# Eight PSUM tiles of one bank behind the attention, and in the attention part a re-planned order and another narrowing of the weights

## The chip, the cores and the metric

One core of one Trainium2 chip runs the whole program in one launch. The metric is the device time of that launch in microseconds (us); a version's time is the median of several runs. The engines are TensorE (PE, with PEld its weight load), VectorE (DVE), ScalarE (ACT), GpSimd (POOL) and SyncE (SP), which only issues DMAs here. They run side by side and wait for each other by semaphores.

## The reference, cut to what matters

The inputs come as float64; the kernel computes in fp32 and in products of two rounded halves.

```python
# q, k, v: (4, 12, 448, 64);  d_model 768;  conv kernel 5;  feed-forward width 3072
def reference(q, k, v, w_val, conv_w, w_out, g_ln, w_ch1, w_ch2):
    x = causal_softmax(q @ k.T / 8) @ v                 # -> (4, 448, 768)
    gate = sigmoid(sum(conv_w[i] * shift(x, 4 - i) for i in range(5)))
    x = (gate * (x @ w_val)) @ w_out
    xn = (x - mean(x)) / sqrt(var(x) + 1e-6) * g_ln
    return x + relu(xn @ w_ch1) @ w_ch2                 # float32
```

## The kernel before

**Four stages follow each other, and each keeps TensorE as full as it can.** The attention stage takes 24 pairs of heads (4 batches of 6). For a pair PE computes the scores (L372, with the last 64 rows in L341 or L347), DVE adds the mask and finds the row maximum (L394), ACT takes exp and the row sum (L400), DVE turns the sums into reciprocals (L403, L404), POOL scales the rows (L408), PE transposes (L443), ACT copies out of PSUM (L446) and PE multiplies with v (L467, L472). The result of a pair goes three ways: ACT copies it to SBUF (L475), POOL splits it into a high and a low half (L238, L479), and DVE runs the convolution over it out of PSUM (L485). When a batch is complete, 36 groups of three products with w_val follow (L599) and DVE multiplies with the gate (L609). These products are laid between the pairs of the next batch; those of the last batch stand alone at the end.

**w_val and w_out are narrowed in this stage.** They arrive as float64, one block of 128 x 768 at a time, 12 blocks in all (`narrow_steps`). The exponent is moved by integer operations on the two 32-bit words: three passes on DVE (L243, L245, L247), an absolute value on ACT (L256), a fourth pass on DVE that zeroes what is too small (L259), then a cast to the high half on ACT (L236) and the low half by a subtraction on POOL (L525).

**The second stage** (`tile_steps`) multiplies 14 tiles of 128 rows with w_out (L812), takes mean and variance on DVE (L827, L835, L836), the inverse root on POOL (L839), keeps the unnormalised row for the residual (ACT L830), normalises (ACT L842), transposes on PE (L848), scales with g_ln on DVE (L851) and forms seven left or right operands of a Strassen-like scheme (L866, L867, sums in L712). **The third stage** multiplies these with w_ch1 (L1038), which is narrowed beside it with a scaled-magnitude variant: ACT L283 takes the absolute value scaled by 2^-112, which is already the shifted exponent, and three DVE passes follow (L264, L266, L268) and no fourth. PSUM sums are copied or added out of PSUM (ACT L1050, DVE L1053), go through a relu on ACT (L1009) and are stored to DRAM by DMAs that ACT issues (L1014). **The fourth stage** multiplies with w_ch2 (L1154); DVE splits its wide weight blocks (L1099) and adds each product to the accumulator (L1165).

**PSUM** has eight banks. Behind the attention they are held as four tiles `Z` of two banks each; the tile's first half and second half are the rings A, B, C of the later stages, and a whole tile is the output `o` of a second-stage tile or its transposed rows `x`.

**The order of the work is written out by a planner.** `Plan.arrange` plays the program through with a cost for each task and engine and picks, at each step, the ready task with the earliest due time. The kernel is then emitted in that order, and every engine and DMA queue works its list in order. The later stages give `lock=True` and a table `TUNE` of shifts to due times, one per kind of task: the planner then also keeps apart tasks marked `hog` on DVE and POOL, and takes pipelining and shorter semaphore hops into account. The attention stage is planned without that, with one due time for each kind of task (`DUE`). `HOME` says for the small sums (L712) whether DVE or POOL takes them.

Of the kernel before, what the change touches and what calls it, by code (L numbers as in the profile page):

```python
# [8 lines left out]
F32 = mybir.dt.float32  # L9
# [17 lines left out]
TUNE = {'eld': -26.4, 'ea': -8.5, 'eb0': 2.2, 'eb1': -4.7, 'es3': -0.8, 'eh0': -6.9, 'eo0': -12.4, 'eh1': 1.6, 'eo1': 22.2, 'es2': -6.7, 'eh2': -9.3, 'eo2': 3.2, 'eh3': -7.7, 'eo3': 10.0, 'eh4': -1.3, 'eo4': 9.9, 'es4': -9.5, 'eh5': -2.9, 'eo5': 22.5, 'eh6': -24.6, 'eo6': 11.2, 'est': 17.6, 'yld': -33.4, 'ylo': 17.2, 'ka': -21.4, 'xst': -15.6, 'km': -1.5, 'kr': 52.9, 'kn': -10.5, 'kt': 0.0, 'fx': 19.4, 'Xh0': 7.8, 'Xl0': 8.6, 'Xh5': -21.6, 'Xl5': 23.0, 'Xt1': -7.7, 'Xh6': 31.9, 'Xl6': 3.3, 'Xh1': 6.1, 'Xl1': 22.0, 'Xt2': -10.7, 'Xh2': -8.2, 'Xl2': 0.0, 'Xt3': -19.7, 'Xt4': -16.1, 'Xh3': -12.7, 'Xl3': 16.1, 'Xh4': -1.1, 'Xl4': 7.2, 'Zh0': 5.7, 'Zl0': -11.5, 'Zh5': -28.2, 'Zl5': -10.8, 'Zh6': 10.5, 'Zl6': -13.0, 'Zh1': 35.6, 'Zl1': -37.2, 'Zt2': 5.3, 'Zh2': -3.9, 'Zt3': -7.3, 'Zt4': -28.4, 'Zh3': 21.6, 'Zl3': -16.3, 'Zh4': 1.4, 'Zl4': -37.8, 'w1ld': -5.7, 'r1': 30.1, 'w0a': 17.9, 'w0b0': -12.7, 'w0b2': -3.0, 'w1a': -3.7, 'w1b0': -22.5, 'w1b1': 48.5, 'w1b2': -4.9, 'ws1': -19.1, 'ws3': -8.1, 'wh0': 3.7, 'wo0': 14.6, 'wh1': 19.8, 'wo1': -10.9, 'ws2': 11.2, 'wo2': 15.3, 'wh3': -5.4, 'wh4': 3.6, 'wo4': -15.0, 'ws4': -19.0, 'wh5': 15.6, 'wh6': -22.4, 'wo6': 16.8, 'r2': 18.1, 'u1a': -5.4, 'u1l': 4.4, 'u1b1': 0.1, 'u0l': 31.4, 'u0b1': -5.2, 'wd5': -4.2, 'wd6': 22.3, 'wd0': -2.9, 'T3': -8.3, 'T1': -19.9, 'T4': 18.6, 'wd3': -28.8, 'wd1': -14.4, 'wd2': -1.6, 'wd4': -4.3, 'cp00': -5.9, 'cp10': 11.5, 'cp20': 14.2, 'ad30': 57.6, 're30': 11.0, 'cp01': -17.8, 'cp21': -28.8, 'ad31': -25.7, 're31': 7.4, 'st31': 5.6, 'ad40': -31.7, 're40': -4.3, 'st40': -15.7, 'ad41': 21.4, 're41': -10.0, 'st41': 0.9, 'ad50': -21.4, 're50': 21.1, 'st50': -15.0, 'ad51': 9.9, 're51': 1.9, 'st51': -2.8, 're60': -3.5, 'st60': 3.9, 're61': 0.1, 'st61': 18.1, 'accld': 29.3, 'sgld': -7.3, 'whi0': -8.5, 'whi1': 16.9, 'wlo1': 14.6, 'whi2': 12.7, 'wlo2': -15.7, 'whi3': -34.1, 'wlo4': -9.1, 'whi5': -6.2, 'wlo5': -5.3, 'whi6': -9.0, 'wlo6': 24.9, 'rld': -18.1, 'sm0': 12.5, 'sm2': 59.3, 'sm3': -4.0, 'clo0': -1.0, 'clo1': 0.3, 'clo2': -7.3, 'clo3': 19.2, 'chi4': 2.8, 'clo4': -42.7, 'chi5': -5.8, 'clo5': -14.6, 'chi6': 8.6, 'clo6': -8.8, 'ac0': 0.4, 'ac1': -15.8, 'ac2': -1.0, 'ac4': -13.6, 'ac5': 43.0, 'ac6': -25.5, 'eb2': 16.3, 'es1': 31.4, 'yhi': -17.3, 'ks': 7.2, 'nm': -7.6, 'Zt1': -3.1, 'Zl2': -14.1, 'w0b1': -1.2, 'wh2': 3.5, 'wo3': 15.4, 'wo5': -5.9, 'u1b0': -21.8, 'u0a': -28.2, 'u0b0': -15.0, 'st30': 15.9, 'cp11': -1.2, 'wlo3': 3.4, 'whi4': -1.3, 'sm1': 0.6, 'chi0': -0.9, 'chi1': 0.2, 'chi2': 30.1, 'chi3': 18.9, 'ac3': 22.8, 'T2': 4.4, 'wlo0': -14.2}  # L27

HOME = {'es1': 'DVE', 'es3': 'POOL', 'es2': 'POOL', 'es4': 'DVE', 'Xt1': 'DVE', 'Xt2': 'DVE', 'Xt3': 'POOL', 'Xt4': 'POOL', 'Zt1': 'POOL', 'Zt2': 'POOL', 'Zt3': 'POOL', 'Zt4': 'DVE', 'ws1': 'POOL', 'ws3': 'DVE', 'ws2': 'POOL', 'ws4': 'POOL', 'T3': 'DVE', 'T1': 'DVE', 'T2': 'DVE', 'T4': 'POOL', 'sm0': 'DVE', 'sm1': 'POOL', 'sm2': 'DVE', 'sm3': 'DVE'}
# [23 lines left out]
class Plan:  # L53
# [6 lines left out]
    SWITCH = 95  # L60
# [21 lines left out]
    def task(self, cost, fn, due, after=(), new=(), uses=(), lag=0, mode=None, hog=False, behind=None, key=None):  # L82
        due += self.tune.get(key, 0)
        if key in self.home:
            cost = {self.home[key]: {'POOL': 1040, 'DVE': 554}[self.home[key]]}

        def run():
            for b in new:
                b.tile = self.place(b)
            fn(k.engine)  # L90

        k = Task(cost, run, due, after, new, uses, lag, mode, hog, behind)
        self.tasks.append(k)
        return k
# [86 lines left out]
def f32(ap):  # L181
    return ap.bitcast(F32)
# [3 lines left out]
def attention_gate_ffn(  # L186
# [98 lines left out]
    with ExitStack() as ph1:  # L285
# [41 lines left out]
        plan = Plan(pools, DUE["same"])  # L327
# [7 lines left out]
        def shared(n, raws, need):  # L335
# [15 lines left out]
            if len(raws) == 1:  # L351
                t = task({"PE": 720}, whole, n + DUE["sc"], need, banks, raws, mode="full")
            else:
                t = task({"PE": 800}, sides, n + DUE["sc"], need, banks, raws, mode="quad")
# [3 lines left out]
        def pair(n):  # L358
# [3 lines left out]
            lq = task({"SP": 900}, dma(lambda: raw.tile, qk[b, c]), n + DUE["lq"], new=[raw], lag=2500)  # L362
            lv = task({"SP": 500}, dma(lambda: v_t.tile, v[b, 2 * c:2 * c + 2].rearrange("h p c d -> p h c d")),
                      n + DUE["lv"], new=[v_t], lag=2500)
# [9 lines left out]
            t01 = task({"PE": 760}, lambda e: scores(e, (0, 1), s01), n + DUE["s01"], [lq, chain["s"]], s01, [raw], mode="row")  # L374
            t2 = task({"PE": 640}, lambda e: scores(e, (2,), s2), n + DUE["s2"], [t01], s2, [raw], mode="row")
# [3 lines left out]
        def weights(n, first, last):  # L379
# [58 lines left out]
            for i, (blocks, need, dst, at) in enumerate(banks):  # L438
# [9 lines left out]
                tt = task({"PE": 440}, turn, n + DUE["turn"] + 0.05 * i, need, [bank], list({b for b, _ in blocks}), mode="full")  # L448
                (tc_ if at is None else te).append(task(
                    {"ACT": 480}, evac, n + DUE["evac"] + 0.05 * i, [tt], [dst] if not at else [], [bank, dst] if at else [bank]))  # L450
            return pt, te, [cpt for _, cpt in ends], tc_

        def rest_of_pair(n, first, own, ends):
# [7 lines left out]
            def attend(e):  # L461
# [6 lines left out]
                for kc in range(NQ + 1):  # L468
                    for h in range(2):
# [4 lines left out]
            ta = task({"PE": 1815}, attend, n + DUE["attend"], [lv, *te, *tc_], [pv], [v_t, pt, *cpts], mode="col")  # L474
            cx = task({"ACT": 430}, lambda e: nc.scalar.copy(x.tile, pv.tile[:, :S]), n + DUE["x"], [ta], [x], [pv])  # L475
            tg = task({"POOL": 610}, lambda e: nc.gpsimd.tensor_scalar(g.tile, x.tile, cw[:, c, KT - 1:KT], 1.0, ALU.mult, ALU.mult),  # L476
                      n + DUE["g"], [cx, tcw], [g], [x])
            th = task({"POOL": 645}, lambda e: cast_hi(xh.tile, x.tile, nc.gpsimd), n + DUE["xh"], [cx], [xh], [x])
            tl = task({"POOL": 1115}, lambda e: nc.gpsimd.tensor_tensor(xl.tile, x.tile, f32(xh.tile), ALU.subtract),  # L479
                      n + DUE["xl"], [th], [xl], [x, xh])  # L480
            last = tg
            for t in range(KT - 1):
# [6 lines left out]
                last = task({"DVE": 715}, conv, n + DUE["conv"] + 0.01 * t, [last], [], [pv, g])  # L489
            return xh, xl, g, tl, last  # L490

        def narrow_steps(c):
# [7 lines left out]
            ld = task({"SP": 3800}, load, due - 0.7, new=[raw], lag=2500)  # L500
# [9 lines left out]
            ops = narrow_ops  # L510

            def bits(i):
                def fn(e):
                    if i == 0:
                        dst["ops"] = ops(raw.tile, w.tile)
# [723 lines left out]
```

## Time and profile before

| what | value |
|---|---|
| median of 3 runs | 1007.7 us (1007.18 to 1008.37) |
| the profiled execution's own time | 1007.35 us |
| its span from first to last instruction | 1005.6 us |
| PE busy, x instructions | 963.7 us (96%), 5731 |
| PEld busy | 857.0 us (85%) |
| DVE busy | 765.0 us (76%), 1549 |
| ACT busy | 561.6 us (56%), 1153 |
| POOL busy | 294.5 us (29%), 367 |

Busy means that an instruction of the engine was under way. A matmul overlaps the one behind it and its end is modelled, so PE busy is no measure of PE at its peak; time in which PE is not busy is a stall for certain. The chain of work that ended last lies on PE for 72% of the span and on DVE for 14%. The granted clock of TensorE was 0.998 of full speed over the span.

### The profile page before, as it was taken

The numbers are of one execution on the slowest core, as the hardware profiler recorded it, in microseconds if no ns is written. First come the engines' busy times: TensorE is split into PE (matmuls) and PEld (weight loads), VectorE is DVE, ScalarE is ACT, GpSimd is POOL, SyncE is SP. The second block draws the span as 40 slices with busy tenths as digits, with TensorE's granted clock in tenths as the row PEclk, the third lists the DMA queues.
The fourth block names the chain that finished last, engine by engine and source line by source line (L and its number), as shares of the span: only waits on it lengthen the run. The fifth ranks groups of instructions, "written<-read, shape, count | busy, mean of one in ns | idle before, by whom it ended". The sixth has DMA issues, their size and how long they took to land.

```text
span 1005.6 us, 16427 instructions
## 1 busy us (share of the span) xinstructions
PE 963.7 (96%) x5731; PEld 857.0 (85%) x5731; DVE 765.0 (76%) x1549; ACT 561.6 (56%) x1153; POOL 294.5 (29%) x367
## 2 busy tenths in 40 slices
PE   9989999999999989999979999999999999999998
PEld 5657777788999978888868878888999999999998
DVE  6899989864488876666667776667999888979873
ACT  7988878862365556666555556564445335334330
POOL 5888877671032231111111121110110000100100
PEclk9999999999999999999999999999999999999999
DMA  6344445322554467878787877689725424424322
GB/s 199 118 158 146 153 154 164 113 83 87 160 173 143 141 225 249 254 222 264 244 251 250 271 223 237 207 265 321 272 84 179 145 63 157 134 82 147 126 95 95
DMA packets 115474, 177.26 MB, mean 176 GB/s; under 512 B 10432, under 2 KB 87744, under 8 KB 115392
## 3 DMA queue, kind: packets, MB, share of 16 engines
q1 hardware_dynamic: 70704, 154.19, 46.3%
q10 hardware_dynamic: 44688, 22.03, 7.5%
q8 instruction: 45, 0.74, 0.3%
q14 instruction: 37, 0.30, 0.1%
HBM read 118.39 MB, written 57.80 MB: 175 GB/s over the span
## 4 chain that ended last, share of the span: by engine, by line
PE 72%; DVE 14%; POOL 4%; DMA 3%; ACT 3%; issue 3%; SPq 0%; ACTq 0%; DVEq 0%; POOLq 0%
PE z L1154 28%; PE z L1038 24%; PE val L599 5%; PE z L812 5%; PE t L443 2%; PE pv L467 2%; PE s L599 2%; DVE g L485 2%; PE s L372 2%; POOL p L408 2%; DVE p L394 1%; DVE x L867 1%; DVE lf L1053 1%; DMA lf<-in_w_ch 1%; DMA hd<-lf 1%
## 5 line engine op out<-in xcount | busy, mean ns | idle before, releaser
L1038 PE MATMUL z<-x,ar 128*128 128x512 f32 (+1 forms) x1224 | 256.5, 368 | 15.4 <-DVE lf L1053 6.3
L1038 PEld LDWEIGHTS z<-x,ar 128*128 128x128 f32 x1224 | 222.9, 189 | 46.5 <-ACT lf L1050 7.9
L712 POOL TENSOR_TENSOR lf<-lf 128x384 f32<-128x384 f32 x52 | 59.4, 1142 | 332.7 <-DVE lf L712 162.3
L1154 PE MATMUL z<-x,x 128*128 128x384 f32 x684 | 125.4, 335 | 1.8 <-DVE lf L1165 0.8
L1165 DVE TENSOR_TENSOR acc<-z,acc 128x384 f32<-128x384 f32 x168 | 91.6, 552 | 46.6 <-PE z L1154 45.4
L1154 PEld LDWEIGHTS z<-x,x 128*128 128x128 f32 x684 | 118.8, 188 | 3.5 <-issue 1.8
L1136 ACT CAST x<-lf 128x384 fp32r<-128x384 f32 x102 | 51.3, 513 | 87.3 <-PE z L1154 67.2
L812 PE MATMUL z<-wo,ar 128*128 128x384 f32 x504 | 91.2, 337 | 0.4 <-DVE ar L801 0.4
L812 PEld LDWEIGHTS z<-wo,ar 128*128 128x128 f32 x504 | 87.0, 188 | 1.1 <-DVE ar L801 0.9
L1154 PE MATMUL z<-x,ar 128*128 128x384 f32 x468 | 85.4, 334 | 0.4 <-ACT ar L1136 0.4
L408 POOL TENSOR_SCALAR p<-p,r 128x128 f32<-128x128 f32 (+1 forms) x144 | 78.4, 567 | 22.4 <-DVE r L404 21.4
L1154 PEld LDWEIGHTS z<-x,ar 128*128 128x128 f32 x468 | 81.4, 188 | 0.7 <-issue 0.7
L400 ACT ACTIVATE p<-p,negm 128x128 f32<-128x128 f32 (+1 forms) x144 | 71.9, 504 | 12.5 <-DVE negm L394 11.7
L485 DVE SCALAR_TENSOR_TENSOR g<-pv,cw,g 128x444 f32<-128x444 f32 (+1 forms) x96 | 64.7, 674 | 11.0 <-POOL g L476 9.0
L1050 ACT COPY lf<-z 128x512 f32<-128x512 f32 (+1 forms) x72 | 37.6, 535 | 52.7 <-PE z L1038 52.0
L1038 PE MATMUL z<-x,w 128*128 128x512 f32 (+1 forms) x288 | 61.8, 366 | 1.4 <-DVE lf L1053 1.4
L1137 DVE TENSOR_TENSOR x<-lf,x 128x384 fp32r<-128x384 f32 x102 | 59.6, 594 | 3.2 <-DMA af<-wd 1.6
L1009 ACT ACTIVATE lf<-lf 128x512 f32<-128x512 f32 (+1 forms) x72 | 41.6, 577 | 36.4 <-DVE lf L1053 32.8
L1038 PEld LDWEIGHTS z<-x,w 128*128 128x128 f32 x288 | 52.4, 188 | 8.6 <-ACT lf L1009 1.8
L1136 ACT CAST ar<-lf 128x384 fp32r<-128x384 f32 x57 | 28.7, 513 | 52.9 <-PE z L1154 43.6
L1053 DVE TENSOR_TENSOR lf<-z,lf 128x512 f32<-128x512 f32 (+1 forms) x72 | 43.5, 618 | 16.5 <-PE z L1038 15.7
L753 DVE TENSOR_TENSOR ar<-lf,ar 128x384 fp32r<-128x384 f32 x62 | 38.1, 619 | 22.8 <-ACT ar L751 22.2
(152 smaller groups left out, 1855.3 us busy)
## 6 DMA issues: line engine op xcount, KB each, us to landing
lf<-in_w_ch SPq DMA_DIRECT2D x31, 768.0 KB, 5.7
af<-wd SPq DMA_DIRECT2D x28, 576.0 KB, 4.9
lf<-hd SPq DMA_DIRECT2D x19, 768.0 KB, 4.4
raw<-in_qk SPq DMA_DIRECT2D x24, 512.0 KB, 4.6
hd<-lf ACTq DMA_DIRECT2D x48, 256.0 KB, 4.1
af<-in_w_ch SPq DMA_DIRECT2D x15, 768.0 KB, 5.2
wd<-af SPq DMA_DIRECT2D x60, 192.0 KB, 3.2
hd<-lf ACTq DMA_DIRECT2D x48, 192.0 KB, 4.5
```

The lines of the kernel that those rows point to most:

```text
L400: nc.scalar.activation(reg, reg, AF.Exp, bias=negm.tile[:, i:i + 1], scale=-1.0, accum_out=ssum.tile[:, i:i + 1])
L408: nc.gpsimd.tensor_scalar(reg, reg, r.tile[:, i:i + 1], 1.0, ALU.mult, ALU.mult)
L485: nc.vector.scalar_tensor_tensor(g.tile[:, d:], pv.tile[:, :S - d], cw[:, c, t:t + 1], g.tile[:, d:], ALU.mult, ALU.add)
L599: nc.tensor.matmul(ps.tile[:, :S], w[:, do, kc * P:(kc + 1) * P], x.tile, start=(kc == 0 and i == 0), stop=(kc == KC - 1 and i == 2),)
L712: ENG[eng].tensor_tensor(o, a, b, op)
L812: nc.tensor.matmul(o.tile[:, nh, :HALF], y.tile[:, kc], wo_t[kc][:, a, nh * HALF:(nh + 1) * HALF], start=(count[nh] == 0), stop=(count[nh] ...
L1038: nc.tensor.matmul(b.tile[:, :width], w.tile[:, a, kc], X[g][p][:, c, kc], start=(m == 0 and fresh), stop=(m == 3 * JJ - 1), skip_group_ch ...
L1053: ka = task({"DVE": 154 + int(1.04 * width)}, lambda e: nc.vector.tensor_tensor(q.tile, b.tile[:, :width], q.tile, ALU.add), t1, [k], [], ...
L1136: k_hi = task({"ACT": 514}, lambda e, src=src, h=h: nc.scalar.copy(h.tile[:, 0], src()), due, [need, k_hi], [h], [buf], key=f"chi{i}")
L1137: k = task({"DVE": 554}, lambda e, src=src, h=h: nc.vector.tensor_tensor(h.tile[:, 1], src(), f32(h.tile[:, 0]), ALU.subtract), due + 1, [ ...
L1154: nc.tensor.matmul(b.tile[:, :HALF], h.tile[:, a, jj], w.tile[:, c, jj], start=(n == 0 and fresh), stop=(n == 3 * JJ - 1), skip_group_chec ...
L1165: k = task({"DVE": 554}, lambda e: nc.vector.tensor_tensor(acc(), b.tile[:, :HALF], acc(), ALU.add), t0 + UNIT + 0.2, [k, acc_ld[u]], [], ...
```

## The change

Five things are changed.

1. In the attention stage the planner is called with `lock=True` and a table `TUNE1` of 267 shifts, one for each kind of task in each batch. The costs of the attention's tasks are other numbers (the row maximum 150 + 1.05 w ns in place of 78 + 1.042 w, exp 385 + 0.81 w in place of 284 + 0.83 w, the reciprocals 390 in place of 310, an evacuation 586 in place of 480, and so on), and the tasks on POOL, the reciprocals and the narrowing are marked `hog`. The order in which the engines get their instructions is thereby another one.
2. `narrow_steps` uses the scaled-magnitude variant of the third stage: one ACT pass (L283's form) and three DVE passes. The ACT absolute value in place and the fourth DVE pass (L256, L259) go.
3. `Z` becomes four pairs of tiles of one bank each. What read or wrote both halves in one instruction is split in two: the copy for the residual (L830), the normalisation (L842) and the scaling with g_ln (L851). The statistics and the transposes address the two tiles.
4. In the planner the small sums cost 1095 ns on POOL in place of 1040, the wide split of L1099 costs 1350 in place of 1260, and a change of PE mode 85 in place of 95.
5. `TUNE` and `HOME` of the later stages are other tables: 164 of 190 shifts differ, and 10 of 24 small sums change engine.

```diff
-    SWITCH = 95
+    SWITCH = 85
...
-            cost = {self.home[key]: {'POOL': 1040, 'DVE': 554}[self.home[key]]}
+            cost = {self.home[key]: {'POOL': 1095, 'DVE': 554}[self.home[key]]}
...
-        plan = Plan(pools, DUE["same"])
+        plan = Plan(pools, DUE["same"], lock=True, tune=TUNE1)
...
-            tr = task({"DVE": 310}, inverse, n + DUE["inv"], tx, [r], [ssum])
+            tr = task({"DVE": 390}, inverse, n + DUE["inv"], tx, [r], [ssum], hog=True, key=f"inv{b}")
...
-                tn.append(task({"POOL": 240 + int(0.83 * w)}, lambda e, a=(i, buf, o, w): norm(e, *a),
-                               n + DUE["norm"] + 0.02 * i, [tr], [], [buf, r]))
+                tn.append(task({"POOL": 230 + int(0.86 * w)}, lambda e, a=(i, buf, o, w): norm(e, *a),
+                               n + DUE["norm"] + 0.02 * i, [tr], [], [buf, r], hog=True, key=f"nrm{b}_{i}"))
...
-            k = ld
-            for i, ns in enumerate((590, 990, 875)):
-                k = task({"DVE": ns}, bits(i), due + 0.01 * i, [k], [w] if i == 0 else [], [raw] if i == 0 else [raw, w], hog=True)
-            ab = task({"ACT": 815}, lambda e: narrow_abs(raw.tile), due + 0.04, [k], [], [raw])
-            k = task({"DVE": 870}, lambda e: narrow_2(raw.tile, w.tile), due + 0.05, [ab], [], [raw, w], hog=True)
-            hi = task({"ACT": 738}, lambda e: cast_hi(parts()[0], w.tile, ENG[e]), due + 0.06, [k], [], [w])
-            lo = task({"POOL": 1800}, lambda e: ENG[e].tensor_tensor(parts()[1], w.tile, f32(parts()[0]), ALU.subtract),
-                      due + 0.07, [hi], [], [w])
+            k = task({"ACT": 915}, lambda e: scaled(raw.tile, w.tile), due - 0.01, [ld], [w], [raw], key=f"na{c // 3}")
+            for i, ns in enumerate((558, 957, 957)):
+                k = task({"DVE": ns}, bits(i), due + 0.01 * i, [k], [], [raw, w], hog=True, key=f"nb{i}_{c // 3}")
+            hi = task({"ACT": 837}, lambda e: cast_hi(parts()[0], w.tile, ENG[e]), due + 0.06, [k], [], [w], key=f"nh{c // 3}")
+            lo = task({"POOL": 1820}, lambda e: ENG[e].tensor_tensor(parts()[1], w.tile, f32(parts()[0]), ALU.subtract),
+                      due + 0.07, [hi], [], [w], hog=True, key=f"no{c // 3}")
...
-        Z = [ps.tile([P, 2, 512], F32, name=f"z{i}") for i in range(4)]
+        Z = [[ps.tile([P, 512], F32, name=f"z{i}_{h}") for h in range(2)] for i in range(4)]
...
-            ka = task({"ACT": 800}, lambda e: nc.scalar.copy(stage.tile.rearrange("p (a f) -> p a f", a=2), o.tile[:, :, :HALF]),
+            def kept(e):
+                for nh in range(2):
+                    nc.scalar.copy(stage.tile[:, nh * HALF:(nh + 1) * HALF], o.tile[nh][:, :HALF])
+
+            ka = task({"ACT": 870}, kept,
...
+            def normed(e):
+                for nh in range(2):
+                    nc.scalar.activation(xn.tile[:, nh * HALF:(nh + 1) * HALF], o.tile[nh][:, :HALF], AF.Identity, bias=nm.tile, scale=rs.tile)
+
+            kn = task({"ACT": 1080}, normed, D(n - 2), [km], [xn], [nm, rs, o], key="kn")
...
+            def scale(e):
+                for q in range(2):
+                    nc.vector.tensor_tensor(fx.tile[:, q], x.tile[q][:, :QU].rearrange("p (c f) -> p c f", f=P),
+                                            g_t[:, q * JJ:(q + 1) * JJ, None].to_broadcast([P, JJ, P]), ALU.mult)
+
+            return task({"DVE": 1024}, scale, D(n - 1), [kt_], [fx], [x], key="fx")
...
-                w_made[kk, i] = task({"DVE": 1260}, lambda e, sg=sg, b=b: nc.vector.tensor_tensor(
+                w_made[kk, i] = task({"DVE": 1350}, lambda e, sg=sg, b=b: nc.vector.tensor_tensor(
```

## Rows read from the trace of the kernel before

**Rows 1.** Busy us (instructions) by stretch: PE, PEld, DVE, ACT, POOL; clock, DMA share, GB/s.

```profile
0.00:20.00 20.00, 17.98 (x81) 10.22 (x83) 14.46 (x68) 14.77 (x50) 10.11 (x25) 1.00 0.67 225
20.00:130.00 110.00, 100.53 (x861) 71.66 (x858) 98.15 (x271) 96.15 (x260) 95.97 (x134) 1.00 0.41 138
130.00:256.00 126.00, 125.28 (x934) 99.62 (x933) 88.28 (x226) 80.98 (x208) 75.76 (x106) 1.00 0.35 119
256.00:357.00 101.00, 96.35 (x580) 94.75 (x578) 80.56 (x164) 56.48 (x92) 25.77 (x28) 1.00 0.50 159
357.00:685.00 328.00, 314.04 (x1520) 275.94 (x1521) 217.57 (x329) 190.52 (x329) 58.11 (x49) 0.99 0.78 245
685.00:1006.00 321.00, 309.54 (x1764) 304.82 (x1762) 266.01 (x494) 122.71 (x219) 28.76 (x27) 1.00 0.42 143
```

**Rows 2.** Chain that ended last, in order of time (start us, us, what): attention's last products.

```profile
233.40 21.91 PE s L599 x108
```

**Rows 3.** Waits of PEld from 20 to 130 us: us in total, times, longest us.

```profile
PEld pv L467 <- DVE g L485: 6.5, 7, 1.5
```

**Rows 4.** Groups of DVE from 20 to 130 us: count, busy us, mean ns, idle before.

```profile
L259 DVE SCALAR_TENSOR_TENSOR wt<-wraw,wt 128x768 f32<-128x768 f32 x7 | 8.0, 1149 | 0.0
...
L245 DVE SCALAR_TENSOR_TENSOR wt<-wraw,wt 128x768 uint32<-128x768 uint32 x6 | 7.2, 1193 | 0.1
...
L403 DVE TENSOR_TENSOR r<-ssum,tiny 128x6 f32<-128x6 f32 (+2 forms) x13 | 5.2, 397 | 0.0
...
L243 DVE TENSOR_SCALAR wt<-wraw 128x768 uint32<-128x768 uint32 x6 | 4.9, 815 | 0.5 <-POOL wvl L525 0.5
```

**Rows 5.** Timeline from 55 to 69 us: start us, us, instruction, idle before and its releaser.

```profile
57.22 1.82 POOL L525 TENSOR_TENSOR wvl<-wt,wvh 128x768 fp32r<-128x768 f32 x1
...
57.75 1.31 DVE L403 TENSOR_TENSOR r<-ssum,tiny 128x8 f32<-128x8 f32 x1
...
59.90 1.51 PE L467 MATMUL pv<-pt,v 128*64 128x384 f32 x12 [1.30 <-DVE g L485]
```

**Rows 6.** The line of the reciprocals over the whole span: ns shortest/median/longest.

```profile
L403 DVE TENSOR_TENSOR r<-ssum,tiny x24: 151/163/1306, 11.2 to 214.0; 128x6 f32<-128x6 f32 x9, 128x8 f32<-128x8 f32 x9, 128x7 f32<-128x7 f32 x6
```

**Rows 7.** Groups by form over the whole span: narrowing passes of either variant.

```profile
L256 ACT ACTIVATE wraw<-wraw 128x768 f32<-128x768 f32 x12 | 11.2, 935 | 0.0
...
L266 DVE SCALAR_TENSOR_TENSOR lf<-lf 128x768 uint32<-128x768 uint32 x15 | 14.3, 956 | 0.3
```

**Rows 8.** Groups by form: the second stage's whole-tile operations and a 384-wide evacuation.

```profile
L1050 ACT COPY lf<-z 128x384 f32<-128x384 f32 x36 | 17.4, 482 | 28.7 <-PE z L1038 28.5
...
L842 ACT ACTIVATE af<-z,nm,rs 128x768 f32<-128x768 f32 x14 | 13.9, 992 | 9.3 <-DVE nm L840 9.3
...
L851 DVE TENSOR_TENSOR af<-z,g_t 128x768 f32<-128x768 f32 x14 | 13.3, 951 | 1.7 <-PE z L848 1.4
...
L830 ACT COPY af<-z 128x768 f32<-128x768 f32 x14 | 11.2, 797 | 3.3 <-issue 2.6 <-DVE st L827 0.5 <-DMA xres<-af 0.2
```

**Rows 9.** Waits from 256 to 357 us: us in total, times, longest us.

```profile
DVE st L827 <- ACT af L830: 6.4, 4, 2.2
...
PE z L1038 <- DVE af L851: 2.9, 1, 2.9
...
PE z L848 <- ACT af L842: 1.4, 1, 1.4
```

**Rows 10.** Timeline of ACT and of PE around 521 us.

```profile
521.11 0.60 ACT L1009 ACTIVATE lf<-z 128x512 f32<-128x512 f32 x1 [3.75 <-DMA wd<-lf]
...
525.91 1.53 PE L1038 MATMUL z<-x,ar 128*128 128x512 f32 x4 [4.45 <-ACT lf L1050]
```

**Rows 11.** Waits of PE over the whole span.

```profile
PE z L1154 <- DVE acc L1165: 4.4, 5, 1.5
```

**Rows 12.** Chain that ended last around 788 us.

```profile
787.90 1.27 DVE x L1099
789.16 0.48 DVE acc L1165
```

More of the change, by code (lines that the diff above doesn't have):

```diff
@@ L32 @@
+HOME = {'es1': 'DVE', 'es3': 'POOL', 'es2': 'DVE', 'es4': 'POOL', 'Xt1': 'DVE', 'Xt2': 'DVE', 'Xt3': 'DVE', 'Xt4': 'DVE', 'Zt1': 'DVE', 'Zt2': 'DVE', 'Zt3': 'POOL', 'Zt4': 'DVE', 'ws1': 'DVE', 'ws3': 'POOL', 'ws2': 'POOL', 'ws4': 'POOL', 'T3': 'DVE', 'T1': 'POOL', 'T2': 'DVE', 'T4': 'DVE', 'sm0': 'DVE', 'sm1': 'POOL', 'sm2': 'DVE', 'sm3': 'DVE'}
 class Buf:
@@ L351, in shared @@
             if len(raws) == 1:
-                t = task({"PE": 720}, whole, n + DUE["sc"], need, banks, raws, mode="full")
+                t = task({"PE": 690}, whole, n + DUE["sc"], need, banks, raws, mode="full", key=f"sh{n // NP}")
             else:
-                t = task({"PE": 800}, sides, n + DUE["sc"], need, banks, raws, mode="quad")
+                t = task({"PE": 850}, sides, n + DUE["sc"], need, banks, raws, mode="quad", key=f"sh{n // NP}")
             chain["s"] = t
@@ L372, in scores @@
                         nc.tensor.matmul(banks[h].tile[:, o:o + W[q]], k[:, q * P:(q + 1) * P], k[:, S:S + W[q]], start=True, stop=True)
-            t01 = task({"PE": 760}, lambda e: scores(e, (0, 1), s01), n + DUE["s01"], [lq, chain["s"]], s01, [raw], mode="row")
-            t2 = task({"PE": 640}, lambda e: scores(e, (2,), s2), n + DUE["s2"], [t01], s2, [raw], mode="row")
+            t01 = task({"PE": 720}, lambda e: scores(e, (0, 1), s01), n + DUE["s01"], [lq, chain["s"]], s01, [raw], mode="row", key=f"sa{b}{c % 2}")
+            t2 = task({"PE": 700}, lambda e: scores(e, (2,), s2), n + DUE["s2"], [t01], s2, [raw], mode="row", key=f"sb{b}{c % 2}")
             chain["s"] = t2
@@ L446, in evac @@
                     nc.scalar.copy(dst.tile if at is None else dst.tile[:, at], bank.tile)
-                tt = task({"PE": 440}, turn, n + DUE["turn"] + 0.05 * i, need, [bank], list({b for b, _ in blocks}), mode="full")
+                tt = task({"PE": 436}, turn, n + DUE["turn"] + 0.05 * i, need, [bank], list({x for x, _ in blocks}), mode="full", key=f"tr{b}_{i}")
                 (tc_ if at is None else te).append(task(
-                    {"ACT": 480}, evac, n + DUE["evac"] + 0.05 * i, [tt], [dst] if not at else [], [bank, dst] if at else [bank]))
+                    {"ACT": 586}, evac, n + DUE["evac"] + 0.05 * i, [tt], [dst] if not at else [], [bank, dst] if at else [bank], key=f"ev{b}_{i}"))
             return pt, te, [cpt for _, cpt in ends], tc_
@@ L487, in conv @@
                     )
-                last = task({"DVE": 715}, conv, n + DUE["conv"] + 0.01 * t, [last], [], [pv, g])
+                last = task({"DVE": 681}, conv, n + DUE["conv"] + 0.01 * t, [last], [], [pv, g], key=f"cv{b}{c % 2}_{t}")
             return xh, xl, g, tl, last
@@ L499, in narrow_steps @@
                 load = dma(lambda: raw.tile, wo_b[c - KC])
-            ld = task({"SP": 3800}, load, due - 0.7, new=[raw], lag=2500)
+            ld = task({"SP": 2330}, load, due - 0.7, new=[raw], lag=2500, key=f"nl{c // 3}")
             dst = {}
@@ L588, in attention_gate_ffn @@
                 gs = [m[2] for m in mine]
-                tgate = task({"ACT": 5400}, lambda e, gs=gs: gates(gs), ready + 0.05, [m[4] for m in mine], [], gs)
+                tgate = task({"ACT": 5400}, lambda e, gs=gs: gates(gs), ready + 0.05, [m[4] for m in mine], [], gs, key=f"gt{b}")
                 tail = b == B - 1
@@ L812, in products @@
                     nc.tensor.matmul(
[L813 removed]
+                        o.tile[nh][:, :HALF], y.tile[:, kc], wo_t[kc][:, a, nh * HALF:(nh + 1) * HALF],
                         start=(count[nh] == 0), stop=(count[nh] == 3 * KC - 1),
@@ L1120, in chain_steps @@
             for i, (o, a, b, op) in enumerate(sums):
-                k = task({"DVE": 554} if i < 2 else {"POOL": 1040}, lambda e, o=o, a=a, b=b, op=op: tt(e, s.tile[:, o], a(), b(), op), due - 19 + i, [ld, k],
+                k = task({"DVE": 554} if i < 2 else {"POOL": 1095}, lambda e, o=o, a=a, b=b, op=op: tt(e, s.tile[:, o], a(), b(), op), due - 19 + i, [ld, k],
                          [] if i else [s], [r, s] if i else [r], hog=True, key=f"sm{i}")
```

76 lines of the change are left out of this document (34 added, 42 removed).

## The prediction

> **What bounds the kernel now.** I read the busy table by stretch first, because one average over four stages says little. TensorE's granted clock is 0.99 to 1.00 in every stretch, so nothing is to be had from the clock [rows 1]. PE is not busy for 2.0 us of the first 20, 9.5 us between 20 and 130, 0.7 us between 130 and 256, 4.7 us in the second stage, 14.0 us in the third and 11.5 us in the fourth: 42.4 us in all [rows 1]. That is the purse this change can draw on, as it takes no product away. The attention ends with 108 products of the last batch from 233.4 to 255.3 us, PE alone [rows 2].
>
> The reader is to see that the attention has two halves. From 130 to 256 PE is 99% busy and nothing on another engine is late. From 20 to 130 no engine is full, but DVE (98.2 of 110 us), ACT (96.2) and POOL (96.0) stand all at 87 to 89% [rows 1]: there the chain from score to exp to reciprocal to scaling to transpose sets the pace, and a long instruction in front of any of its links is seen by PE. Who releases PEld there shows it: first of all the convolution on DVE, 6.5 us in 7 times [rows 3]. A weight load waits sooner than its product does, and its part of these waits can lie under the product before, so they bound PE's loss from above; together with the smaller ones of the same view (18 lines, of which those put down to issue are left out) they come to some 20 us, and 9.5 is the bound from below.
>
> **Where that time goes.** In 20 to 130 us DVE spends 8.0 us in seven fourth passes of the narrowing (L259), 7.2 us in six L245 and as much in L247, 5.2 us in thirteen L403 [rows 4]. L245's counterpart in the third stage, where the planner keeps POOL and DVE apart, takes 956 ns [rows 7] against 1193 here. The reason stands in one place of the timeline: L525 on POOL runs from 57.22 for 1.82 us, to 59.04; the reciprocals' first operation L403, eight numbers a row, starts at 57.75 and ends at 59.06, 1.31 us, and the product with v at 59.90 comes 1.30 us late behind it [rows 5]. The two engines hold each other up, and the link of the softmax chain pays.
>
> **The change part by part.** First the narrowing. Per block it takes away L259 and L256 and adds one scaled absolute value on ACT, which is the same kind of operation as L256 at 935 ns [rows 7]: nothing more on ACT. On DVE 12 passes go. Of these, 7 lie between 20 and 130 us and are worth 8.0 us there; the other 5 lie where PE is 99% busy, and I count them at nothing: PE's products hide them [rows 1, 4]. If that cover were gone they would be worth 5 x 1.15 = 5.7 us more. The upper end for this part is 8.0 + 5.7 = 13.7. The lower is a loss: the first step now stands on ACT, and if a block came late, ACT would hold the exps queued behind it, and PE the scores' successors. Before, DVE was in that place, and L243 waited 0.5 us for POOL and for no DMA [rows 4], so the blocks come in time; I put 1 us there, twice what L243 waited.
>
> Second the order of the attention. If it keeps L403 from starting under a POOL operation, the 13 of that half cost their median of 0.163 us each [rows 6], so up to 5.2 - 13 x 0.163 = 3.1 us come off the chain [rows 4]. The other stretched passes would give 2 x (7.2 - 6 x 0.956) = 2.9 us of DVE time, which is not on the chain by itself [rows 4, 7]. What is gained is taken from PE's idle time in that half, 9.5 us by its own busy time and some 20 by its loads' waits, so 8.0 + 3.1 = 11.1 us fits between the two, and I take it. Ends: 4 us more than before (three new stalls of 1.30 us, as in rows 5, and nothing gained) and 18 us less (nearly all of the 20). What is late next: ACT, which has 96 us of work in that stretch and gets none taken away, and POOL with 96.
>
> Third the eight tiles. Splitting costs instructions. ACT's 384-wide copy out of PSUM takes 482 ns, so the 797 ns copy becomes at most 964, and the 992 ns normalisation and DVE's 951 ns scaling get about the same 0.17 us more [rows 8]. That is 14 x 3 x 0.17 = 7.1 us over both engines at the most. In that stage ACT has 56.5 us of 101 to do and DVE 80.6 [rows 1]; it lies beside PE's products, and I count it at nothing; without that cover it would cost the chains of the first and the last tile 0.34 us each. The gain: DVE's statistics wait four times for ACT's copy out of the same two banks, 6.4 us in all [rows 9], and with halves each waits for half. DVE is not what PE waits for there but twice: the first product of the third stage comes 2.9 us late behind L851, and a transpose 1.4 us behind L842 [rows 9]. The bank that the first product needs is free after half of L851, 0.48 us sooner, and the first three transposes can start after half of L842, 0.5 us sooner. That is 1.0 us; ends +0.7 (both chains, nothing gained) and -4.3 (both waits gone).
>
> Fourth the new tables of the later stages. They change the place of nearly every instruction on ACT, DVE, POOL, SP and of the DMAs that ACT and SP issue, and no product. The profile of before can't show the new order, so bounds: all 25.5 us of PE's idle time in stages three and four gone, or as much again added [rows 1]. The row nearest is that of the fourth stage where PE waits for the addition out of PSUM, 4.4 us in five times [rows 11]; ahead of the addition at 789.16 stands a split of 1.27 us, L1099 [rows 12], whose cost in the planner was 1.26 against 1.35 in the new table. A plan that knows it to be longer sends the addition first. I take these 4.4 us and leave the rest as it is.
>
> **The sum.** 1007.35 (the profiled execution, whose span is 1005.6, with 1.75 us around it) - 11.1 - 1.0 - 4.4 = 990.9 us. The profiled execution stands 0.35 us under the median of the runs, which is less than I can foresee: 991.
>
> **The rivals.** (a) *POOL and ACT hold the attention.* POOL 95.97 and ACT 96.15 of 110 us stay as they are [rows 1]. If the reciprocals no longer wait for POOL, POOL's operations wait for DVE instead, and only half of the 8.0 us of removed passes reaches PE; the later stages' new order comes out even. Then 1007.35 - 4.0 - 1.0 = 1002. For it: POOL's and DVE's numbers are as high as each other's. Against it: a DVE pass that is gone frees POOL too.
>
> By the Trainium skill, page "SBUF — State Buffer", section "Who interferes with whom", a DVE operation with two SBUF inputs and a GpSimd operation that reads SBUF share one port pair as an exclusive lock, and the one that comes second waits for the whole of the other. The stall in rows 5 (1.31 us for eight numbers a row, over when POOL is) agrees. By that rule an order can choose who waits but not make the wait vanish, which is rival (a).
>
> (b) *Much more.* PE's idle time in the attention was nearer 20 us than 9.5, and the new order takes 18; the third and fourth stages lose half of their 25.5, 12; the second 2. 975 us. For it: the waits of the loads [rows 3]. Against it: two independent things have to go well.
>
> (c) *Slower.* In the third stage ACT issues the stores of the relu's results itself, and a buffer that is not yet stored holds ACT's whole list: at 521.11 ACT had waited 3.75 us for a DMA, and PE's next product came 4.45 us late, because the evacuation stood behind the relu [rows 10]. DMAs are busy for 0.78 of that stage [rows 1]. Before, this happened once at this size. If the new order, which moves every load and store on SP's and ACT's queues, makes it happen k times more, the price is 4.45 k. From k = 4 on (16.5 / 4.45 = 3.7) the change is no gain; with k = 5 the time is 991 + 22 = 1013.
>
> (d) *Nothing.* The attention's new order starts from as many late links as the old one, the removed pass only lengthens DVE's idle time: 1007 us.
>
> **How the numbers follow.** The forecast gets 0.50, with its own range 983 to 1000 (the attention's gain between 6 and 14, that of stages three and four between 0 and 9); (a) 0.20; (b) 0.13; (c) 0.13; (d) 0.04. Measurements of this kernel tell a change from none at about 0.2%, or 2 us. Faster is the forecast, (a) and (b): 0.83; within that bound (d): 0.04; slower (c): 0.13. The range reaches from (b) to between (a) and (c), 975 to 1008, and leaves about half of (b) and most of (c) out.
>
> **What would show it.** The last product of the attention ends near 244 us in place of 255.3; a value over 251 proves the second half of step one wrong, and under 238 proves (b). No L403 is longer than 0.6 us. DVE is busy about 14 us less up to the attention's end, and POOL's busy time there falls too, as its operations wait less; if POOL's doesn't fall, (a). The second stage is 1 us shorter, and the statistics wait less than 3.2 us for the copy. PE's idle time is about 14 us in the third stage and 7 in the fourth; a third stage with over 25, and ACT waiting for DMAs in it, is (c). The prediction is wrong as a whole if the attention's end moves by less than 4 us or the later stages' idle time changes by more than 12.

## The result, and the profile after

The changed kernel takes 973.8 us (median of 4 runs, 971.6 to 974.19) against 1007.44 before: a ratio of 0.9661, 95% interval 0.9644 to 0.9677. I had forecast 991, range 975 to 1008. The direction was right, the gain is twice what I said, and most of it lies elsewhere.

The table gives each stage's length in the profiled execution, from the start of its first product to that of the next stage's (for the fourth, to the start of its last product), in us, for all kernels of this study. The attention ends where the second stage's first product starts.

| kernel | attention ends | second | third | fourth | median, ratio to before |
|---|---|---|---|---|---|
| before | 255.1 | 101.8 | 327.8 | 317.0 | 1007.4 |
| after | 249.9 | 101.2 | 311.5 | 306.0 | 973.8, 0.9661 |
| tiles_only | 254.9 | 101.0 | 310.7 | 305.6 | 979.5, 0.9721 (0.9694 to 0.9748) |
| after_two_bank | 250.2 | 101.9 | 330.7 | 315.7 | 1004.3, 0.9976 (0.9956 to 0.9996) |
| split_ac | 249.8 | 101.5 | 315.1 | 310.1 | 983.3, 0.9764 (0.9743 to 0.9786) |
| split_ab | 250.3 | 101.6 | 321.8 | 312.8 | 994.1, 0.9867 (0.9847 to 0.9887) |
| attention_only | 250.2 | 102.1 | 328.4 | 316.9 | 1003.3, 0.9955 (0.9935 to 0.9975) |
| old_tables | 249.9 | 102.5 | 311.0 | 305.6 | 974.9, 0.9685 (0.9669 to 0.9702) |
| narrowing_only | 257.0 | 101.9 | 329.8 | 316.9 | 1008.5, 1.0012 (1.0000 to 1.0025) |
| fourth_pass | 258.0 | 101.3 | 310.2 | 307.5 | 982.4, 0.9750 (0.9732 to 0.9767) |
| two_passes | 249.4 | 101.0 | 308.9 | 306.9 | 973.2, 0.9665 (0.9648 to 0.9682) |
| no_shifts | 265.3 | 101.0 | 310.0 | 306.0 | 983.9, 0.9772 (0.9743 to 0.9801) |

The profiled executions lie within 2.1 us of the medians but for two: no_shifts took 988.0 us in it (4.1 above its median) and narrowing_only 1011.2 (2.7 above), so for these two I go by the medians where it matters.

Of the 33.1 us that the last product comes sooner, 5.3 are the attention's, 0.6 the second stage's, 16.3 the third's and 10.9 the fourth's. The busy table of the changed kernel by stretch (columns as in [rows 1], the cuts at its own stages) shows it:

```profile
0.00:20.00 20.00, 17.17 (x87) 10.02 (x89) 12.58 (x66) 15.11 (x49) 9.05 (x25) 1.00 0.66 226
20.00:130.00 110.00, 107.66 (x893) 74.26 (x890) 89.69 (x275) 100.22 (x275) 86.98 (x135) 1.00 0.47 153
130.00:249.00 119.00, 118.32 (x890) 94.26 (x889) 79.34 (x209) 76.83 (x194) 71.03 (x104) 1.00 0.33 113
249.00:351.00 102.00, 97.97 (x588) 96.31 (x586) 84.35 (x189) 58.99 (x117) 9.95 (x16) 1.00 0.48 157
351.00:667.00 316.00, 315.99 (x1545) 282.38 (x1546) 229.60 (x338) 194.77 (x335) 56.73 (x48) 0.99 0.82 259
667.00:973.00 306.00, 301.68 (x1739) 301.07 (x1738) 265.72 (x490) 119.05 (x214) 31.97 (x27) 1.00 0.43 146
```

PE had 14.0 us of idle time in the third stage [rows 1] and has none now. The chain of work that ended last (start us, us, what) runs through that stage and the fourth in a few long pieces on PE, where that of before changed engine dozens of times:

```profile
356.50 306.14 PE z L1045 x1503
662.64 4.69 PE z L1161 x27
...
675.29 293.56 PE z L1161 x1692
```

Three of PE's waits in the later stages (engine, line, released by: us, times, longest); the only other is one of 0.2 us, and the 4.4 us of [rows 11] are 0.2 as well:

```profile
PE z L1045 <- DVE af L857: 2.8, 1, 2.8
...
PE z L852 <- ACT af L846: 1.1, 1, 1.1
...
PE z L1161 <- DVE acc L1172: 0.2, 1, 0.2
```

### The profile page after: what moved, and what is told of

Same layout as the page of the kernel before. It is cut to its first block, busy times and chain, and to the rows that moved or that the text cites. A ratio compares the mean times of both kernels' runs of the same rounds, so it can differ in the third digit from the quotient of the medians.

```text
span 972.4 us, 16420 instructions
## 1 busy us (share of the span) xinstructions
PE 958.8 (99%) x5731; PEld 858.3 (88%) x5731; DVE 761.3 (78%) x1565; ACT 565.0 (58%) x1181; POOL 265.7 (27%) x353
## 4 chain that ended last, share of the span: by engine, by line
PE 63%; DVE 2%; issue 0%; ACT 0%
PE z L1045 32%; PE z L1161 31%; DVE x L874 0%; DVE st L825 0%; DVE af L710 0%; DVE acc L1172 0%; DVE x L1144 0%; DVE af L857 0%; PE z L852 0%; DVE x L1106 0%; DVE lf L1172 0%; DVE ar L799 0%; ACT ar L238 0%; ACT af L846 0%; DVE lf L710 0%
## 5 line engine op out<-in xcount | busy, mean ns | idle before, releaser
L710 POOL TENSOR_TENSOR lf<-lf 128x384 f32<-128x384 f32 x52 | 62.0, 1193 | 322.7 <-DVE lf L710 274.2
L402 ACT ACTIVATE p<-p,negm 128x128 f32<-128x128 f32 (+2 forms) x144 | 72.1, 503 | 9.1 <-DVE negm L396 7.6
L410 POOL TENSOR_SCALAR p<-p,r 128x384 f32<-128x384 f32 (+2 forms) x144 | 70.8, 508 | 17.1 <-DVE r L406 12.7
L751 DVE TENSOR_TENSOR ar<-lf,ar 128x384 fp32r<-128x384 f32 x62 | 35.8, 582 | 32.1 <-ACT ar L749 32.0
L396 DVE CUSTOM_DVE_ANT_0 p<-s,mask 128x128 f32<-128x128 f32 (+2 forms) x144 | 52.4, 417 | 5.9 <-PE s L374 3.5
```

The costliest lines, as they stand in the source:

```text
L396: nc.vector.tensor_tensor_reduce(buf.tile[:, o:o + w], bank.tile[:, at:at + w], m, NEG_SCALE, 3.0e38, ALU.add, ALU.min, negm.tile[:, i:i + 1])
L402: nc.scalar.activation(reg, reg, AF.Exp, bias=negm.tile[:, i:i + 1], scale=-1.0, accum_out=ssum.tile[:, i:i + 1])
L410: nc.gpsimd.tensor_scalar(reg, reg, r.tile[:, i:i + 1], 1.0, ALU.mult, ALU.mult)
L710: ENG[eng].tensor_tensor(o, a, b, op)
```

## The experiments

**Which part made the later stages shorter.** There are two theories. T says that a two-bank tile makes work on one half wait for work on the other. P says that the stalls come from the order that the old tables give. The first kernel has the tiles without the tables, the second the tables without the tiles.

```diff
 # tiles_only: before, with
-        Z = [ps.tile([P, 2, 512], F32, name=f"z{i}") for i in range(4)]
+        Z = [[ps.tile([P, 512], F32, name=f"z{i}_{h}") for h in range(2)] for i in range(4)]
 # and kept, normed, scale as in the change; planner's costs and tables of before
 # after_two_bank: after, with
-        Z = [[ps.tile([P, 512], F32, name=f"z{i}_{h}") for h in range(2)] for i in range(4)]
+        wide = [ps.tile([P, 2, 512], F32, name=f"z{i}") for i in range(4)]
+        Z = [[w[:, h] for h in range(2)] for w in wide]
```

tiles_only. 

> The kernel before with the eight one-bank tiles and the three split operations alone; planner, costs, tables and so the order of the tasks are those of before. Theory T (tiles): with two-bank tiles a product into one half waits for readers of the other half, and that made the stalls of the third and fourth stage (327.8 and 317.0 us before, 311.5 and 306.0 after). Then these two stages shorten by 15 to 27 us in sum and the time is 980 to 993 us. Rival P (plan): the stalls come from the order that the old tables give. Then the two stages stay within 5 us of before and the time is 1001 to 1009 us.

after_two_bank. 

> The changed kernel with four two-bank tiles under the same eight views; order, split operations and all tables are those of the changed kernel. Theory T: the stalls come back, the third and fourth stage are 12 to 27 us longer than in the changed kernel, 986 to 1001 us. Rival P: within 4 us of the changed kernel, 972 to 978 us. Both: the attention ends at 250 us as in the changed kernel.

Both came out as T says. The tiles alone take 28.4 us off the third and fourth stage (644.7 to 616.3) and bring the time to 979.5. The changed kernel with two-bank tiles has 646.4 us in these stages, 28.9 more than the changed kernel and 1.7 more than before, which has the old tables. Its time, 1004.3 us, lies 3.3 us past what I had written for T: under two-bank tiles the new tables are no better than the old. PE waits for the same kinds of instructions as before again (us in total, times, longest):

```profile
PE z L1046 <- ACT lf L1058: 9.5, 9, 2.3
PE z L1046 <- DVE lf L1061: 6.9, 5, 2.4
PE z L1162 <- DVE acc L1173: 4.1, 6, 0.9
```

**How a half waits for the other.** I followed one stall of the kernel before, at 427 us, and the same unit of work in tiles_only, where all engines have the same order. A unit is nine products into one bank. The third stage goes through w_ch1 in visits; i counts the seven units of a visit, and each is done for two groups of rows, the first 512 and the second 384 columns wide. In the kernel before, the unit of visit 2, i = 2, second group, goes into the first half of Z0 and ends at 421.55 (where the next one starts); the next unit goes into the second half of Z0 and ends at 423.63. ACT's copy out of the first half is the third line here (timeline of ACT, kernel before):

```profile
418.68 0.90 ACT L283 ACTIVATE lf<-af 128x768 f32<-128x768 f32 x1
420.15 0.59 ACT L1050 COPY lf<-z 128x512 f32<-128x512 f32 x1 [0.57 <-PE z L1038]
423.82 0.48 ACT L1050 COPY lf<-z 128x384 f32<-128x384 f32 x1 [3.08 <-PE z L1038]
424.19 0.90 ACT L283 ACTIVATE lf<-lf 128x768 f32<-128x768 f32 x1
```

and here in tiles_only, where that unit ends at 418.87:

```profile
415.98 0.90 ACT L283 ACTIVATE lf<-af 128x768 f32<-128x768 f32 x1
417.44 0.59 ACT L1059 COPY lf<-z 128x512 f32<-128x512 f32 x1 [0.57 <-PE z L1047]
419.03 0.48 ACT L1059 COPY lf<-z 128x384 f32<-128x384 f32 x1 [1.00 <-PE z L1047]
419.41 0.89 ACT L283 ACTIVATE lf<-lf 128x768 f32<-128x768 f32 x1
```

With one-bank tiles the copy starts 0.16 us behind its unit. With two-bank tiles it starts 2.27 us behind it, and 0.19 us behind the unit in the other half. Everything behind it in ACT's list slips by two microseconds: the narrowing's L283, and through it DVE's passes and the additions behind them. Then the wait comes back to PE. This is the kernel before again, DVE and PE (timeline, in two fences):

```profile
427.05 0.96 DVE L268 SCALAR_TENSOR_TENSOR lf<-lf 128x768 uint32<-128x768 uint32 x1
427.93 1.15 DVE L1053 TENSOR_TENSOR lf<-z,lf 128x384 f32<-128x384 f32 x2
```

```profile
422.69 4.76 PE L1038 MATMUL z<-x,ar 128*128 128x512 f32 x22
429.23 1.80 PE L1038 MATMUL z<-x,ar 128*128 128x384 f32 x9 [1.77 <-DVE lf L1053]
```

The unit at 429.23 goes into the first half of Z0, whose last reader was the copy above, done at 424.30. It is released by DVE's additions, and the second of these reads the second half of Z0. In tiles_only PE runs through the same place without a stop. So the reader waits for the writer of the other half, and the next writer for the other half's reader. Nothing here points to a limit of the banks: after and after_two_bank have the same instructions in the same order, and only the declaration of the tiles differs. That the wait stands in the semaphores, which the program would then get for a whole tile, is concluded from this and was not tested by itself.

**If that is so, half the tiles cure their own half of the stalls.** With four two-bank tiles (after_two_bank) I noted for each stall of the third stage the bank that the late product goes into: 8 at ring C, 11.7 us, and 6 at ring B or the second group's A, 7.0 us; every one stands at the first product of a unit. A ring is a set of banks that are used in turn. Z1 and Z3 hold ring C beside the first group's banks of ring A, Z0 and Z2 ring B beside the second group's.

```diff
 # split_ac: split = (1, 3); split_ab: split = (0, 2)
+        for i in range(4):
+            if i in split:
+                Z.append([ps.tile([P, 512], F32, name=f"z{i}_{h}") for h in range(2)])
+            else:
+                w = ps.tile([P, 2, 512], F32, name=f"z{i}")
+                Z.append([w[:, 0], w[:, 1]])
```

split_ac. 

> The changed kernel with only Z1 and Z3 as one-bank tiles (they hold ring C beside half of ring A) and Z0 and Z2 as two-bank tiles (ring B beside the other half of A). Theory T: of the stalls with four two-bank tiles, those at products into ring C go (8 in the third stage, 11.7 us, and 2 of 0.95 us in the fourth), those at ring B and the second group's A (7.0 us in the third) stay: the third stage 317 to 321 us against 330.7, the time 988 to 993 us. Rival D (any two-bank tile slows every product, or only all eight help): both half splits give the same, the third stage 320 to 322 us each, or no gain in either.

split_ab. 

> The other half: Z0 and Z2 as one-bank tiles, Z1 and Z3 two-bank. Theory T: the stalls at ring B and at the second group's A go, 7.0 us of the third stage, those at ring C stay: the third stage 322 to 326 us against 330.7, the time 994 to 999 us, so less than the other half. Rival D: as with the other half.

split_ac: the third stage takes 315.1 us, 15.6 less than with four two-bank tiles. The stalls at ring C are gone. Of the five that are left, three (0.8 to 2.5 us) stand at ring B and the second group's A and wait for evacuations on DVE and ACT. The other two are not of this kind: one at ring B waits 0.9 us for a load, and one of 0.5 us at a first group's A waits for a narrowed weight. It gained 4 us more than the sum of its stalls and came out 2 us under the range that I had written; a stall at C that also fed others would explain it, which was not followed up. split_ab: 321.8 us, 9.0 less, and all six stalls that are left (0.8 to 2.65 us) stand at ring C. Rival D is out: the two halves differ by 6.7 us, each as its rings have it. PE's waits in split_ac, then in split_ab:

```profile
PE z L1052 <- DVE lf L1067: 3.1, 2, 2.4
...
PE z L1168 <- DVE acc L1179: 1.2, 3, 0.6
```

```profile
PE z L1052 <- ACT lf L1064: 8.5, 5, 2.5
PE z L1168 <- DVE acc L1179: 3.8, 4, 1.6
```

**Are the new tables worth anything with the new tiles?** old_tables has the changed attention and tiles, and the planner's costs and tables of before for the later stages.

```diff
-            cost = {self.home[key]: {'POOL': 1095, 'DVE': 554}[self.home[key]]}
+            cost = {self.home[key]: {'POOL': 1040, 'DVE': 554}[self.home[key]]}
 # and TUNE, HOME and the later stages' costs as in before
```

> The attention part and the eight tiles of the changed kernel, but the planner's costs and the tables TUNE and HOME of the later stages as in the kernel before. Theory T: the tables brought nothing, the second to fourth stage take 617 to 618 us as with the tiles alone (618.6 in the changed kernel), 971 to 975 us in all. My prediction's step (the new tables are worth 4.4 us): 977 to 980 us.

974.9 us, with 619.0 us from the second to the fourth stage against 618.6 in the changed kernel. The tables are worth nothing that these runs can tell. Stage by stage they do two small things. The granted clock was 0.99 in the third stage of the changed kernel's profile, but 1.00 in the third and fourth of two_passes, which has the same later stages, and of tiles_only, which has the old tables. Between these two, the new tables take the third stage from 310.7 to 308.9 us and the fourth from 305.6 to 306.9.

**The attention.** attention_only sets the changed attention before the later stages of before; narrowing_only puts the new narrowing into the planner of before.

```diff
 # narrowing_only: before, with
-            ab = task({"ACT": 815}, lambda e: narrow_abs(raw.tile), due + 0.04, [k], [], [raw])
-            k = task({"DVE": 870}, lambda e: narrow_2(raw.tile, w.tile), due + 0.05, [ab], [], [raw, w], hog=True)
+            k = task({"ACT": 815}, lambda e: scaled(raw.tile, w.tile), due - 0.01, [ld], [w], [raw])
 # ahead of the three passes, which are those of merged
```

attention_only. 

> The attention part of the changed kernel (new order and new narrowing) before the later stages of the kernel before, with its tiles and tables. All theories: the attention ends 5 us sooner (255.1 to 250 us), the later stages are as before, 1001 to 1004 us; if the later stages change by more than 3 us, the stages aren't separable.

narrowing_only. 

> The kernel before with the scaled-magnitude narrowing alone; the planner with its old costs and no lock places three DVE passes and one ACT pass per block instead of four and one. Theory N (the removed DVE pass is what the attention gained): the attention ends 3.5 to 6 us sooner, 1001 to 1004 us. Rival O (the new order is what it gained): at most 2 us sooner, 1005 to 1008 us. My prediction had put 8.0 us on the pass alone: 999 us.

attention_only came as expected: the attention ends at 250.2 us, the later stages are within 1 us of before. narrowing_only did not gain at all: the time is 1.0012 of before, and in its profiled execution, at a clock of 0.98 between 20 and 130 us, the attention ends 1.9 us later. So the 12 passes that went bought nothing in the order that the old planner makes around them.

Then the price of a pass in the new order, one more and one fewer (two_passes leaves out the one that puts the signs in), and the order without its shifts:

```diff
 # fourth_pass: after, with, behind the third pass,
+                    if i == 2:
+                        wu = w.tile.bitcast(U32)
+                        nc.vector.scalar_tensor_tensor(wu, raw.tile[:, :, 1], 0x80000000, wu, ALU.bitwise_and, ALU.bitwise_or)
 # two_passes: after, with
-                    next(dst["ops"])
+                    if i < 2:
+                        next(dst["ops"])
 # no_shifts: after, with
-        plan = Plan(pools, DUE["same"], lock=True, tune=TUNE1)
+        plan = Plan(pools, DUE["same"], lock=True)
```

fourth_pass. 

> The changed kernel with a repeated third DVE pass in each of the 12 narrowings of the attention (12 x 0.96 us more on DVE, the result the same), the order otherwise that of the changed kernel. My prediction's step (a DVE pass between 20 and 130 us is worth its length): the attention ends 5 to 8 us later than 250. Rival S (DVE has slack there, and the scoring chain passes beside the narrowing): at most 2 us later. Later stages unchanged, 974 to 982 us.

two_passes. 

> The changed kernel without the third DVE pass of the narrowing in the attention (the signs of w_val and w_out are left out of the computation); 12 x 0.96 us less on DVE, the order otherwise the same. Theory D (a DVE pass in this order still costs what the fourth did, 0.66 us each): the attention ends 5 to 8 us sooner, at 242 to 245 us. Rival E (PE and its mode changes are what is left): at most 2 us sooner, 248 to 250 us, 971 to 974 us in all.

no_shifts. 

> The changed kernel with the table of shifts of the attention (TUNE1) left empty: lock, the new costs and the new narrowing stay. Theory C (costs and lock make the order better): the attention ends at 249 to 252 us, 973 to 977 us in all. Rival H (the shifts carry the gain): the attention ends at 254 us or later, 978 us or more.

fourth_pass ends the attention 8.1 us later: 0.68 us for each of 12. two_passes ends it 0.5 us sooner, and its median is 0.6 us lower: next to nothing. The new order has room for three passes, and most of one pass more stands in the chain. The planner did not know of the added pass, so what an order made for four would cost is not shown. no_shifts ends the attention at 265.3 in its profiled execution; by the medians it is 10.1 us slower than with the shifts, so the attention ends at 260 to 265 and later than before (255.1): lock, costs and the new narrowing without the 267 shifts make a worse order than the old one, and the shifts carry the gain. The busy tables (columns as in [rows 1]) from 20 to 130 us, first fourth_pass, then two_passes, agree: PE is busy 104.6 of 110 us with four, 107.5 with two, as with three.

```profile
20.00:130.00 110.00, 104.55 (x848) 71.03 (x845) 93.05 (x278) 96.61 (x264) 88.12 (x132) 1.00 0.45 146
```

```profile
20.00:130.00 110.00, 107.50 (x892) 74.50 (x889) 82.65 (x268) 100.55 (x274) 85.01 (x136) 1.00 0.49 156
```

## Why the prediction was right or wrong

**Step four failed, and step three with it.** I put the third and fourth stages' stalls down to the order, said that the new tables would take 4.4 us of them, and counted the tiles at 1.0 us, all in the second stage; what the tiles do for the later stages I put at nothing without a reason. These stages lost 27.2 us, and tiles_only, after_two_bank, split_ac, split_ab and old_tables show that the tiles took them, all but one wait of 1.6 us (rival (c) below). The new tables are worth about 1 us (974.9 with the old against 973.8), in place of 4.4. I had priced the tiles only in the second stage, where instructions touch both halves [rows 9], and did not ask whether the rings A, B and C of the later stages, whose banks are separate, share a tile. By the sign that I had set for it the prediction is wrong as a whole: PE's idle time in these stages changed by far more than 12 us, from 25.5 [rows 1] to 4.3. About 4 us of either figure lie behind the last product, where no order can take them; I had counted them in. The trace of before held the answer in a line I had not weighed: ACT's copies in the third stage had waited 52.0 us for PE in 40 times, the longest 3.1 us, in a stage where a unit takes 1.6 to 2.1 us. This is that line (us in total, times, longest), and under it its successor in the changed kernel:

```profile
ACT lf L1050 <- PE z L1038: 52.0, 40, 3.1
```

```profile
ACT lf L1057 <- PE z L1045: 35.9, 42, 1.8
```

With one-bank tiles the longest such wait is 1.8 us here and 1.9 in tiles_only (2.3 in old_tables); one of 3.1 us has to be looked at. What settles it is its end, 0.19 us behind the unit in the other half.

**The stall that I read as a late split** ([rows 12]: L1099 ahead of the addition) was of the same kind. The split takes no less (1.38 us on average, 1.35 before), and PE's wait for the addition fell from 4.4 to 0.2 us. With two-bank tiles it is 4.4 us under the old tables and 4.1 under the new; in tiles_only, with the old tables, PE has no such wait.

**Step one and two, the attention, 11.1 us, measured 5.3.** The mechanism holds in part. L259 is gone, the reciprocals' first operation takes 3.1 us in place of 5.2 between 20 and 130 us, L268 959 ns in place of 1193. These are the changed kernel's lines (as in [rows 4]):

```profile
L270 DVE SCALAR_TENSOR_TENSOR wt<-wraw,wt 128x768 uint32<-128x768 uint32 x7 | 7.0, 1006 | 0.1
L268 DVE SCALAR_TENSOR_TENSOR wt<-wraw,wt 128x768 uint32<-128x768 uint32 x7 | 6.7, 959 | 0.1
...
L405 DVE TENSOR_TENSOR r<-ssum,tiny 128x6 f32<-128x6 f32 (+2 forms) x14 | 3.1, 221 | 0.4 <-ACT cp L402 0.4
```

PE's idle time between 20 and 130 us went from 9.5 to 2.3 us. What was mis-sized is what it is worth: I took a pass's whole length off the path whatever the order, while a fourth pass costs 0.68 us each time in the new order, and taking it out gains nothing in narrowing_only. Part of the gain PE gives back: up to the attention's end its idle time fell by 6.4 us, but its busy time rose by 1.1. It changes more often between tasks whose operands have other shapes (the kernel marks them with `mode`: full, row, quad or col), 136 times in place of 107, and a transpose with another mode behind it takes 0.09 us longer than one with a transpose behind it (0.20 against 0.11). By that, 29 more changes would cost 2.7 us (an estimate; 1.1 were measured). Its loads' waits put down to issue, the largest four lines of the first 250 us, are 27.6 us now and were 24.6. These are the lines of after:

```profile
PEld pv L469 <- issue: 10.8, 55, 0.5
PEld t L445 <- issue: 7.0, 19, 0.7
PEld s L374 <- issue: 5.5, 25, 0.7
...
PEld val L597 <- issue: 4.3, 7, 0.7
```

That the changes of shape are what costs PE this time was argued from the trace and not tested. Since two_passes gained next to nothing, PE's own list is the bound there, or ACT's (100.2 of 110 us); which of the two stays open. My "No L403 is longer than 0.6 us" fell: the longest of L405, its successor, takes 0.96.

**Step three in its own stage was near in size, and partly by luck.** The second stage is 0.6 us shorter (1.0 forecast), but the two waits that I had counted on lost 0.4 us between them: the one ahead of the third stage went from 2.9 to 2.8, that of the transpose from 1.4 to 1.1, where I had put 0.5 on each. The split copy takes 12.5 us busy in place of 11.2, the normalisation 17.2 in place of 13.9, the scaling 14.3 in place of 13.3 [rows 8]: 5.6 us more where I had bounded 7.1, all hidden. These are after's lines:

```profile
L846 ACT ACTIVATE af<-z,nm,rs 128x384 f32<-128x384 f32 x28 | 17.2, 665 | 2.0 <-DVE nm L842 2.0
L857 DVE TENSOR_TENSOR af<-z,g_t 128x384 f32<-128x384 f32 x28 | 14.3, 549 | 1.9 <-PE z L852 1.8
L830 ACT COPY af<-z 128x384 f32<-128x384 f32 x28 | 12.5, 481 | 9.1 <-issue 6.6 <-DVE st L825 2.6
```

The statistics no longer wait for ACT's copy (6.4 us in [rows 9]); it waits for them, 2.6 us. The first product of the third stage still waits for L857, the scaling.

**The rivals.** (a) is right in that the removed pass alone bought nothing, and wrong in all else: 1002 was 28 us too high, and POOL's busy time up to the attention's end fell from 181.8 to 167.1 us; had it not fallen, that was to be the sign of (a). With the reciprocals' shorter time this says that the new order made the two engines wait less for each other, and did not only choose which of them waits. (b)'s 975 is nearly the time, for a wrong reason: the attention gave 5 and not 18, the later stages 27 and not 12. (c), ACT held by a store as at 521 us [rows 10], did not come in the changed kernel: PE has no such wait in its third stage. With the old order it does come, also with one-bank tiles. These are ACT and PE in tiles_only, at the same unit as at 525.91 before (timeline):

```profile
513.35 0.60 ACT L1018 ACTIVATE lf<-z 128x512 f32<-128x512 f32 x1 [4.65 <-DMA wd<-lf]
```

```profile
515.95 2.25 PE L1047 MATMUL z<-x,ar 128*128 128x512 f32 x8 [1.62 <-ACT ar L751]
```

The DMA that these lines name is the one that landed last. ACT goes on at 512.88 with the issue of a store, just behind the landing (512.80) of a store that it had issued itself at 504.32; before, these times are 520.64, 520.57 and 511.69. ACT is held no shorter than before, but PE's product comes 1.62 us late in place of 4.45. So the tiles took most of this stall and the new order the rest, which is about what the third stage gains from the new tables.

## What to carry to other kernels

Price a tile's shape by every pair of instructions that touch any part of it, not by the banks: here two-bank tiles cost 28 us of 1007, by waits between instructions that worked on different banks. In this trace the sign was a reader of PSUM that waited longer than the unit it reads took to write and was released as another unit ended. And a removed instruction is worth what the order around it makes of it: taking 12 passes out gained nothing in the old order, and in the new one 8.1 us from four to three and 0.5 from three to two.

## What was not expected

PE can run 1503 and 1692 products in a row without one wait on another engine while DVE is busy for 230 of 316 us and ACT for 195: with this load on them the later stages are not bound by DVE or ACT. And in the new order of the attention DVE's work has a cliff and hardly a slope: 12 passes more cost 8.1 us, 12 fewer gain 0.5.
